# Moving the next chunk's projections, its norm and the FFN within the steps of an in-order transformer schedule

## The chip, the cores and the metric

One core of a Trainium2 chip. The metric is the device time of the whole kernel in microseconds (us), the median over its runs.

## The reference, cut to what matters

```python
# S = 2048 rows, D = 512, H = 32 heads of 16, window W = 256, Dff = 1792
def A(x):                                    # attention over a sliding window
    q, k, v = split_heads(x @ wqkv)
    scores = q @ k^T * Dh ** -0.5, masked to 0 <= i - j < W
    return (softmax(scores) @ v) @ wo
def B(x):
    return relu(x @ w1) @ w2
x = x + A(layernorm(x));  x = x + B(layernorm(x))
x = x + A(layernorm(x));  x = x + B(layernorm(x))
```

## The kernel before

The rows are cut into four chunks of 512, so two layers make eight **steps** (`k` from 0 to 7). A step has 20 **slots** (`SPS = 20`), each with one group of scores, one exponential on ACT (the scalar engine) and the matching product with V. POOL (GpSimd) and DVE (the vector engine) do masks, norms and evictions, that is, moves of results out of the matmul accumulator memory PSUM. In the gaps the tensor engine (PE) does the dense work: output projection and FFN of the chunk that is finished (`k - 1`), and the projections of the chunk that comes next (`k + 1`). Each compute engine gets its instructions in exactly the order in which the program emits them; SyncE (its issuing sequencer is SPq in the profile) issues the DMAs, also in order.

Dense work is a list of tasks. In each slot the task with the smallest `due` among those with `early <= slot` is taken, until the slot's budget of matmuls is spent; once begun, a task is finished before the next.

```python
    def plan_qkv(k, early, w0, w1):
        ...
        order = ["K0", "Q0", "V0", "K1", "V1", "Q1", "V2", "K2", "V3", "Q2", "K3", "Q3"]
        for i, what in enumerate(order):
            n = int(what[1])
            due = w0 + (w1 - w0) * (i + 1) / len(order)
            if what[0] == "K":
                Task(early, due, SPS * k + 5 * n - 3, KC, lambda n=n: k_items(layer, c, xnTs[k], n, k == 0))
            ...                                        # Q and V likewise
    # in the loop over k:
        for j in range(4):                             # norm of the next chunk, in two pairs of blocks
            at_slot(SPS * k + 5 + j, lambda k=k, j=j, fn=begin: fn(k, j))
        plan_qkv(k + 1, SPS * k + 9, SPS * k + 9, SPS * k + 20)
```

Three kinds of DMA matter. A **K group** (four in a step) leaves PSUM by ACT into a staging tile `Kst` with two buffers, and eight small copies put it into the block-diagonal `KBD`. `KBD` is a ring of 20 places: where a chunk wraps round its end (chunks 2 and 7, projected in steps 1 and 6), a group takes 16 copies. That makes 5 x 32 + 2 x 64 = 288 copies in the run. The first chunk (`direct`) is written by DVE without copies.

```python
            if not direct:
                Kst = work.tile([P, 512], BF16, name="Kst", bufs=2)
                act.copy(Kst[:], ps[0][:])
            for a, b in runs:                          # one run, or two where the ring wraps
                sa = (s0 + a) % NSLOT
                for e in range(2):
                    if direct:
                        dve.tensor_scalar(out=KBD[:, t, sa:sa + b - a, e, :], in0=ps[0]..., scalar1=par[:, e:e + 1], op0=ALU.mult)
                        continue
                    for r in range(4):
                        rows = slice(32 * r + 16 * e, 32 * r + 16 * e + 16)
                        nc.sync.dma_start(KBD[rows, t, sa:sa + b - a, e, :], Kst[rows, 64 * a:64 * b]...)
```

A **V group** (four in a step) goes by DVE to one of two staging tiles `Vst`, then by four copies to `V2f`: 112 in the run. The third kind are the **transposes**: the attention output to `OT` (four in a step, ahead of the output projection `wo`), the second norm to `xn2T` (four, ahead of the FFN) and the chunk norm to `xnT` (four, ahead of the projections). `xnT` and `xn2T` have one buffer each.

## Time and profile before

| | before |
|---|---|
| time, median of 2 runs | 674.69 us (672.6 to 676.79) |
| span, mean granted clock of the profiled run | 673.0 us, 0.844 |
| busiest engine | PE, 75% |
| K copies, V copies, transposes issued | 288, 112, 92 |

The prediction below shows how the bound was read. The "chain" in it is the work that ended last, followed back step by step to what released it; a line such as "PE 46%; SPq 12%" gives the share of the run that each engine has in that chain.

### The profile page before, as it was taken

To read this page: it belongs to the slowest core of one execution; us is meant where nothing else is said; L and a number is where in the kernel's file an instruction comes from. 1 tells how busy PE (TensorE), PEld (TensorE's weight loads), DVE (VectorE), ACT (ScalarE), POOL (GpSimd) and SP (SyncE) were. 2 spreads that over 40 slices of the span, in tenths; PEclk is the share of its full clock that TensorE was granted. 3 is DMA by queue.
4 is the path that set the end of the run, shared out by engine and by line. 5 is a ranking of instruction groups with operands and counts; after the bars stand their busy time and mean duration, and the time that the engine had idled before them with its cause. 6 is when DMAs were issued, how large, how long until landed. Compare 5 with 4: busy or idle time off the path is not lost.

```text
span 673.0 us, 14446 instructions
## 1 busy us (share of the span) xinstructions
PE 507.5 (75%) x5741; PEld 239.7 (36%) x5741; DVE 333.7 (50%) x869; ACT 317.9 (47%) x223; POOL 253.3 (38%) x558
## 2 busy tenths in 40 slices
PE   5929454797376996599958996799859586697395
PEld 2314232343132552244423442255325243344142
DVE  5662344453173646456554656364826216463451
ACT  2355673474234774367524674377626273453000
POOL 6652245431135344632453235334453221432300
PEclk8768665797786999899977997699969697699788
DMA  8511212111121112211121212112221112102201
GB/s 293 175 31 26 38 30 56 23 23 27 34 41 35 36 28 54 43 25 37 32 56 34 38 36 56 29 34 46 56 50 19 27 20 60 38 9 41 47 1 37
DMA packets 101244, 30.64 MB, mean 46 GB/s; under 512 B 85552, under 2 KB 100656, under 8 KB 101168
## 3 DMA queue, kind: packets, MB, share of 16 engines
q1 hardware_dynamic: 101168, 29.63, 20.0%
q8 instruction: 47, 0.77, 0.5%
q14 instruction: 29, 0.24, 0.1%
HBM read 7.86 MB, written 2.10 MB: 15 GB/s over the span
## 4 chain that ended last, share of the span: by engine, by line
PE 46%; DVE 14%; SPq 12%; POOL 9%; DMA 9%; issue 5%; ACT 3%; DVEq 0%; POOLq 0%; ACTq 0%
PE ps_d L94 35%; SPq L244 10%; PE acc L94 6%; PE Sps L94 5%; DMA OT<-O 4%; ACT Pb L94 3%; SPq L266 3%; DMA xnT<-xnA 3%; POOL Pb L94 3%; DVE stB L94 2%; POOL xnB L94 2%; DVE x_sb L94 2%; DVE stA L94 2%; POOL xnA L94 1%; DVE Pb L94 1%
## 5 line engine op out<-in xcount | busy, mean ns | idle before, releaser
L94 ACT ACTIVATE Pb<-Sps 128x2048 bf16<-128x2048 f32 (+2 forms) x160 | 283.4, 1771 | 207.4 <-PE Sps L94 193.3
L94 POOL TENSOR_SCALAR_AFFINE_SELECT Pb<-Pb 64x256 bf16<-64x256 bf16 x368 | 153.8, 418 | 244.5 <-ACT Pb L94 198.4
L94 PE MATMUL ps_d<-xn2T,w 128*128 128x512 bf16 x448 | 131.6, 416 | 40.8 <-DMA xn2T<-xnB 27.0
L94 DVE TENSOR_SCALAR hT<-ps_d 128x512 bf16<-128x512 f32 x112 | 77.3, 690 | 96.8 <-PE ps_d L94 96.4
L94 PE MATMUL ps_d<-w,hT 128*128 128x512 bf16 x448 | 115.9, 390 | 0.0
L94 PEld LDWEIGHTS <-Pb 128*128 128x128 bf16 x2880 | 94.0, 98 | 38.5 <-issue 14.1
L94 PE MATMUL ps_d<-xnT,wqkv 128*128 128x512 bf16 x256 | 80.9, 429 | 32.0 <-issue 16.4
L94 PE MATMUL acc<-V2f,Pb 128*128 128x34 bf16 x2880 | 95.9, 181 | 2.3 <-DVE Pb L94 1.5
L94 PE MATMUL Sps<-Qt,KBD 32*128 32x320 bf16 (+4 forms) x1408 | 67.2, 275 | 26.8 <-ACT Pb L94 25.8
L94 PE MATMUL ps_d<-wo,OT 128*128 128x512 bf16 x128 | 43.8, 470 | 48.9 <-DMA OT<-O 48.9
L94 DVE RECIPROCAL chk<-acc 128x8 f32<-128x8 f32 x128 | 26.1, 204 | 96.7 <-PE acc L94 96.0
L94 PEld LDWEIGHTS <-w 128*128 128x128 bf16 x448 | 40.2, 102 | 94.1 <-issue 57.3
L94 DVE TENSOR_TENSOR Pb<-Pb,tri 128x512 bf16<-128x512 bf16 (+1 forms) x152 | 60.4, 430 | 6.7 <-ACT Pb L94 6.5
L94 PEld LDWEIGHTS <-KBD 32*128 32x128 bf16 x1408 | 25.4, 95 | 93.1 <-issue 90.2
L94 PEld LDWEIGHTS <-hT 128*128 128x128 bf16 x448 | 38.9, 99 | 46.5 <-issue 11.4
L94 DVE TENSOR_TENSOR x_sb<-ps_d,x_sb 128x512 f32<-128x512 f32 x48 | 32.6, 688 | 43.4 <-PE ps_d L94 41.5
L94 POOL TENSOR_TENSOR rstdB<-rstdB,mhalf 128x2 f32<-128x2 f32 x16 | 11.7, 731 | 103.9 <-DVE rstdB L94 103.9
L94 ACT CAST Kst<-ps_d 128x512 bf16<-128x512 f32 x28 | 16.3, 583 | 70.8 <-PE ps_d L94 63.9
L94 PEld LDWEIGHTS <-wqkv 128*128 128x128 bf16 x256 | 23.5, 103 | 62.2 <-issue 46.0
L94 DVE TENSOR_TENSOR O<-acc,chk 128x128 bf16<-128x128 f32 x128 | 37.3, 292 | 4.4
L94 PE MATMUL ps_d<-wqkv,xnT 128*128 128x512 bf16 x128 | 36.9, 391 | 0.0
L94 DVE CAST Vst<-ps_d 128x512 bf16<-128x512 f32 x28 | 19.4, 692 | 32.3 <-DMA V2f<-Vst 25.5
(66 smaller groups left out, 253.0 us busy)
## 6 DMA issues: line engine op xcount, KB each, us to landing
V2f<-Vst SPq DMA_DIRECT2D x112, 34.0 KB, 1.9
w<-in_B_w_dram SPq DMA_DIRECT2D x2, 1792.0 KB, 13.7
KBD<-Kst SPq DMA_DIRECT2D x160, 16.0 KB, 1.9
KBD<-Kst SPq DMA_DIRECT2D x128, 8.0 KB, 1.8
out_dram<-ob SPq DMA_DIRECT2D x16, 128.0 KB, 1.7
wqkv<-in_A_wqkv_dram SPq DMA_DIRECT2D x3, 512.0 KB, 6.9
xst<-in_A_x_dram SPq DMA_DIRECT2D x3, 512.0 KB, 9.8
xst<-in_A_x_dram SPq DMA_DIRECT2D x2, 256.0 KB, 3.0
```

The lines of the kernel that those rows point to most:

```text
L94: inst = fn(*a, **k)
L244: nc.sync.dma_start(KBD[rows, t, sa:sa + b - a, e, :], Kst[rows, 64 * a:64 * b].rearrange("p (s k) -> p s k", k=64))
L266: nc.sync.dma_start(V2[64 * e:64 * e + 64, sl, e].rearrange("p a d -> p (a d)"), Vst[j % 2][64 * half:64 * half + 64, e].rearrange("p a d ...
```

## The change

The intent is to have the next chunk's projections done early, in the first half of a step, where PE has idle time; to leave the second half to the FFN of the finished chunk; and to run the next chunk's norm at the end of the step before, so that its transposes are not waited for. The diff, cut to its core:

```diff
-    def plan_qkv(k, early, w0, w1):
+    def plan_qkv(k, base):
...
-        order = ["K0", "Q0", "V0", "K1", "V1", "Q1", "V2", "K2", "V3", "Q2", "K3", "Q3"]
+        order = [("K0", 1), ("K1", 2.5), ("K2", 4), ("K3", 5.5), ("Q0", 7), ("V0", 8), ("V1", 9), ("V2", 10), ("V3", 11),
+                 ("Q1", 12.5), ("Q2", 14.5), ("Q3", 17)]
...
-                Task(early, due, SPS * k + 5 * n - 3, KC, lambda n=n: k_items(layer, c, xnTs[k], n, k == 0))
+                Task(base, base + due, base + SPS + 5 * n - 3, KC, lambda n=n: k_items(layer, c, xnTs[k], n, k == 0))
...
-        w0, w1_ = SPS * (k + 1) + 9, SPS * (k + 2) + 9          # FFN
+        w0, w1_ = SPS * (k + 1) + 9, SPS * (k + 2) + 8
...
-            at_slot(SPS * k + 5 + j, lambda k=k, j=j, fn=begin: fn(k, j))
-        plan_qkv(k + 1, SPS * k + 9, SPS * k + 9, SPS * k + 20)
+            at_slot(max(2 + j // 2, SPS * k - 4 + j), lambda k=k, j=j, fn=begin: fn(k, j))
+        plan_qkv(k + 1, SPS * k)
```

More of the change, by code (lines that the diff above doesn't have):

```diff
@@ L460, in q_make @@
             return q_items(xnTs[k], Q[k, t], t, k == 0)
-        order = ["K0", "Q0", "V0", "K1", "V1", "Q1", "V2", "K2", "V3", "Q2", "K3", "Q3"]
-        for i, what in enumerate(order):
+        order = [("K0", 1), ("K1", 2.5), ("K2", 4), ("K3", 5.5), ("Q0", 7), ("V0", 8), ("V1", 9), ("V2", 10), ("V3", 11),
+                 ("Q1", 12.5), ("Q2", 14.5), ("Q3", 17)]
+        if k == 0:
+            order = [("K0", 0), ("Q0", 0), ("V0", 1), ("V1", 1), ("V2", 1), ("V3", 1), ("K1", 2), ("Q1", 2), ("K2", 5),
+                     ("Q2", 5), ("K3", 8), ("Q3", 8)]
+        for what, due in order:
             n = int(what[1])
-            due = w0 + (w1 - w0) * (i + 1) / len(order)
             if what[0] == "K":
-                Task(early, due, SPS * k + 5 * n - 3, KC, lambda n=n: k_items(layer, c, xnTs[k], n, k == 0))
+                Task(base, base + due, base + SPS + 5 * n - 3, KC, lambda n=n: k_items(layer, c, xnTs[k], n, k == 0))
             elif what[0] == "Q":
-                Task(max(early, SPS * (k - 1) + 5 * n + 1), due, SPS * k + 5 * n - 1, KC, lambda n=n: q_make(n))
+                Task(base + 5 * n + 1 if k else 0, base + due, base + SPS + 5 * n - 1, KC, lambda n=n: q_make(n))
             else:
-                Task(max(early, SPS * (k - 1) + 7), due, SPS * k + 3, KC, lambda n=n: v_items(layer, c, xnTs[k], n, k == 0))
+                Task(base + 7 if k else 0, base + due, base + SPS + 3, KC, lambda n=n: v_items(layer, c, xnTs[k], n, k == 0))
     def plan_ffn(k, s):
@@ L519 @@
         pool.tensor_copy(x_sb[:, b, :], xst[:, b - 4, :])
-    plan_qkv(0, 0, 0, 6)
+    plan_qkv(0, -SPS)
     for k in range(NSTEP - 1):
```

## The prediction

> **What bounds the kernel now.** The schedule has eight steps (two layers, four chunks of 512 rows), each of 20 attention slots; an exponential per slot marks them, so I call the start of every twentieth one a step. From their starts in the timeline the steps of the kernel before last 60.7, 77.2, 84.5, 72.5, 69.9, 73.3, 80.7 and, with the tail, 124.9 us. I read the page first (busy shares, chain), then the list of waits, then windows of one ordinary step (245.2 to 317.7 us) cut at its slot 10, and last that step's timeline.
>
> ```profile
> span 673.0 us, 14446 instructions
> PE 507.5 (75%) x5741; PEld 239.7 (36%) x5741; DVE 333.7 (50%) x869; ACT 317.9 (47%) x223; POOL 253.3 (38%) x558
> PE 46%; DVE 14%; SPq 12%; POOL 9%; DMA 9%; issue 5%; ACT 3%; DVEq 0%; POOLq 0%; ACTq 0%
> ```
>
> No engine is full. A sixth engine shows in the chain: SPq, the sequencer that issues every DMA, with 12%.
>
> ```profile
> 245.20:289.10 43.90, 30.66 (x375) 14.48 (x374) 21.91 (x61) 20.22 (x13) 21.10 (x44) 0.88 0.21 41
> 289.10:317.70 28.60, 28.60 (x375) 14.27 (x375) 18.19 (x43) 21.43 (x16) 10.18 (x24) 1.00 0.18 32
> ```
>
> Columns: length, then PE, PEld, DVE, ACT and POOL busy, the granted clock, DMA share, GB/s. From slot 10 on PE is busy all the time at full clock, 28.6 us: nothing can be gained there. The first half holds the waits: 43.90 - 30.66 = 13.2 us of idle PE, at clock 0.88. The waits by name, over the run (us in total, times, longest):
>
> ```profile
> PE ps_d L94 <- DMA OT<-O: 48.9, 12, 10.5
> PE ps_d L94 <- DMA xn2T<-xnB: 27.0, 7, 9.6
> DVE Vst L94 <- DMA V2f<-Vst: 25.5, 5, 9.2
> PE ps_d L94 <- DMA xnT<-xnA: 15.0, 3, 7.6
> ACT Kst L94 <- DMA KBD<-Kst: 4.5, 2, 3.8
> ```
>
> And in that step's timeline (start, us, engine, work, idle before):
>
> ```profile
> 268.89 0.61 PE L94 MATMUL ps_d<-wo,OT 128*128 128x512 bf16 x1 [5.23 <-DMA OT<-O]
> ...
> 280.11 1.04 PE L94 MATMUL ps_d<-xn2T,w 128*128 128x512 bf16 x4 [2.76 <-DMA xn2T<-xnB]
> ...
> 285.70 1.01 PE L94 MATMUL ps_d<-xnT,wqkv 128*128 128x512 bf16 x2 [4.55 <-issue]
> ...
> 288.89 5.10 SPq L244 DMA_DIRECT2D KBD<-Kst  x8
> ...
> 303.17 6.00 SPq L266 DMA_DIRECT2D V2f<-Vst  x8
> ```
>
> Three transposes in turn stop PE: OT (attention output, to wo), xn2T (to the FFN), xnT (to the next chunk's projections): 12.5 of the 13.2 us. The last two lines give the price of issuing: 5.10/8 = 0.64 us for one K copy, 6.00/8 = 0.75 for one V copy (0.62 in most groups of four); transposes in the same timeline take 1.25 us each to issue. A copy lands some 1.25 us after its issue ended.
>
> **What the Trainium skill says.** "Perfetto Trace Analysis", What "DMA-bound" means: a kernel can be bound on the DMA sequencer, when the issuing engine's track is solid DMA slices, and these slices are descriptor generation, not data movement. The trace agrees: the 16 engines are 20% busy, but a step issues 32 K copies (21 us), 16 V copies (10 us) and 12 transposes (15 us), 46 of some 72 us of SPq. "DMA: Bandwidth & Descriptors", Anatomy of one DMA — SWDGE (gpsimd) path: a wait for a semaphore happens on the issuing sequencer, before dispatch. So a copy whose source isn't ready holds all later ones; SPq's waits show it. "PSUM — Partial Sum Buffer", Engine vs sequencer instructions: ScalarE, VectorE and GpSimdE are strict FIFO; so an eviction that waits for a buffer holds every exponential behind it. The waits of ACT and DVE above are of this kind. "TensorE: Matmul & The Clock Gate", Part 1: after about 3.4 us of idle PE the clock halves. The trace's clock is 1.0 or 0.5 alone, and the waits stand in the windows with 0.82 to 0.88.
>
> **The change, part by part.** No work is added or removed. The instruction order of the changed kernel, compared engine by engine, says what moves.
>
> 1. The chunk norm goes from slots 5 to 8 to the last slots of the step before. That removes the xnT wait (4.55 us above, about 4 a step) and lets the fourth OT transpose go ahead of xn2T's first pair. By the order, xnT lands about 1 to 2 us into the step, just before its first use.
>
> 2. FFN starts its second matmuls in slot 15, so by slot 0 most are done, and the projections are pulled forward: in steps 1 to 6 all four K groups are in slots 0 to 2, where K was spread over slots 9 to 19 with V and Q between. Kst has two buffers. K0 and K1 are evicted at about 5 and 5.5 us; K2's eviction waits for K0's eight copies to land: 5.6 + 8 x 0.66 + 1.2 = 12.1 us; K3's for K1's, 17.4 us. ACT is in order: the exponential of slot 3 comes behind K3, at 18.6 us, where it stood at 8.4.
>
> 3. SPq's new order is K0 K1 (16), OT0, K2 K3 (16), OT1 to OT3, xn2T (4), V (16). OT0 lands at 16.2 + 2.4 = 18.6 us, hidden behind part 2. K2 and K3 issue until 28.1; OT1 lands at 30.5, OT3 at 33.1, where before it landed at 23.7. Slot 6 starts at 33 (before: 17.4).
>
> 4. From the last wo on: addition, statistics, POOL, xn and transposes take 9 to 10 us (5.5 of DVE and POOL durations, 2.5 issue, 1.2 landing, some queueing). xn2T lands at 43.8 and PE has done slots 7 and 8 by then.
>
> 5. V's groups are in slots 7 and 8, but their copies stand behind xn2T, until 42.5. Vst has two buffers: V2's eviction waits until 42.5 + 2.5 + 1.25 = 46.3, V3's until 48.8, and DVE is in order, so the accumulators of slot 8 and the first relu wait too. PE has four such PSUM tiles: its second FFN group waits for V2's, its third for V3's. Slot 10 starts at about 50.5 (before: 43.9).
>
> 6. From slot 10 on nine large matmuls a slot as before: 28 us. An ordinary step: 50.5 + 27.5 = 78 us, with step 4 (smaller exponentials) 76.
>
> 7. Split steps 1 and 6: the ring wraps, and each K takes 16 copies, 64 in all, 42 us. Step 1 has 48 ahead of OT0: K2 can be evicted at 14.6, K3 at 25.1, OT0 lands at 37, OT1 at 48.5 (16 more). Its OT3 also stands behind xn2T's first pair: 59. Last wo 60, xn2T 68.5, V until 73.5, slot 10 at 75.5: step 103 us. Step 6 (32, OT0, 32): OT3 at 53.7, xn2T 64.4, slot 10 at 71: 98 us. In return step 2 loses the spill of step 1's copies (84.5 becomes 78), and step 7, which projects nothing, that of step 6's: it had a slot of 11.9 us behind them; slots 0 to 8 now take 24 us, xn2T is there at 29, eleven slots of 3.15 follow: 64 for 71.8.
>
> 8. Step 0: K0 of the next chunk is in slot 4, but xnT has one buffer, so its transposes wait for the last Q of this chunk: 13 us, plus 5 issuing, plus 1.2. K copies issue from 21 to 42 us, V after that; V3's eviction is at 48.6, two units of 11 us are left: 70 (before 60.7).
>
> Sum of differences: step 0 +9.3, step 1 +25.8, step 2 -6.5, steps 3 to 5 +5.5 +6 +5, step 6 +17.5, step 7 -8: **+54.6 us on 674.7, 729 us**. All these times are estimates by hand from the durations above.
>
> **The rivals.** (a) The intended gain: the transposes' waits vanish and nothing replaces them. For it: PE's three waits in the list make 91 us; the norm does leave the critical place. Against: the OT and xn2T waits depend on SPq, and its order puts all K copies before OT. If half of the 91 us went, 629. (b) A trade at par: K's burst fills time in which PE has other work, as ACT has slack (47% busy), and the lost xnT wait pays for the rest. For it: first-half PE work is only some 30 of 43.9 us. Against: wo and FFN depend on each other, there are just 72 matmuls to put in between, and those stand in order behind the wait. It would give 665 to 690. (c) Worse than the sum: longer idle stretches halve the clock for more of the first half, and DVE, behind by 5 us at slot 10, keeps FFN groups waiting for PSUM. 750 to 765.
>
> **Range and chances.** I trust the sign: it comes from the order on a queue whose durations are measured. The size hangs on the split steps (43 of the 55 us) and on step 0. If half of the K burst were hidden, 700; with (c), 760. So 729, 8 in 10 in 698 to 760; faster 0.04, same 0.06, slower 0.90.
>
> **What would show it.** Right: waits of Kst for KBD grow from 4.5 us to over 60 (in an ordinary step 4 + 5, in a split one about 8 + 10, each with its 20 us or so of late exponentials); Vst for V2f from 25.5 to about 40; the OT wait from 48.9 to 70 or more; xnT below 10; steps 1 and 6 near 100 us, steps 2 and 7 shorter; no group's mean duration changed but by the clock. Wrong: steps 1 and 6 not longer than 85 us, or a first half below 44 us with K's copies still ahead of OT; then copies issue faster when the queue is full than the groups of eight show, or the evictions don't wait.

## More of the kernel before

Besides, two lines of the table of DMA issues and two of the table of groups are needed later. The first two give the tiles, the count, the size and the time from issue to landing; the others give count, busy us, mean ns, and after the second bar the idle time before the group and what ended it.

```profile
KBD<-Kst SPq DMA_DIRECT2D x160, 16.0 KB, 1.9
KBD<-Kst SPq DMA_DIRECT2D x128, 8.0 KB, 1.8
...
L94 PE MATMUL ps_d<-wo,OT 128*128 128x512 bf16 x128 | 43.8, 470 | 48.9 <-DMA OT<-O 48.9
...
L94 ACT CAST Kst<-ps_d 128x512 bf16<-128x512 f32 x28 | 16.3, 583 | 70.8 <-PE ps_d L94 63.9
```

The reader should see that ACT's evictions of K wait for the matmuls that make K, not for copies: before the change the staging buffers are nearly always free in time.

## The result, and the profile after

The changed kernel took 774.21 us (median of 2 runs, 773.59 to 774.82) for 674.69. A ratio in this text is the mean time of one kernel's fast runs over the mean of the fast runs of the kernel before from the same rounds, so not quite the ratio of the two medians. Here it is 1.1475, with a 95% interval of 1.1316 to 1.1633: slower by some 15%. The experiments' own runs of the kernel before had medians of 674.1 to 674.9 us.

The page of the kernel after, in the same order as the lines of before in the prediction and above: span, busy time, engines of the chain that ended last, then the two groups.

```profile
span 773.1 us, 14419 instructions
...
PE 527.7 (68%) x5741; PEld 242.7 (31%) x5741; DVE 330.2 (43%) x869; ACT 317.1 (41%) x223; POOL 254.2 (33%) x558
...
PE 36%; SPq 22%; POOL 12%; DVE 11%; DMA 9%; issue 6%; ACT 3%; ACTq 0%; DVEq 0%; POOLq 0%
...
L94 PE MATMUL ps_d<-wo,OT 128*128 128x512 bf16 x128 | 49.8, 541 | 102.6 <-DMA OT<-O 102.2
...
L94 ACT CAST Kst<-ps_d 128x512 bf16<-128x512 f32 x28 | 16.0, 587 | 98.3 <-DMA KBD<-Kst 79.3
```

The counts are the same, 5741 matmuls and 28 evictions of K, and DVE, ACT and POOL are busy for the same time within 4 us. PE alone is busy 20 us longer, with the same instructions: its mean clock fell from 0.844 to 0.807. The issuing sequencer's share of the chain rose from 12% to 22%. The waits by name:

```profile
PE ps_d L94 <- DMA OT<-O: 102.2, 15, 18.2
ACT Kst L94 <- DMA KBD<-Kst: 79.3, 14, 9.7
DVE Vst L94 <- DMA V2f<-Vst: 53.8, 8, 13.0
PE ps_d L94 <- DMA xnT<-xnA: 33.1, 7, 9.7
PE ps_d L94 <- DMA xn2T<-xnB: 25.4, 7, 10.0
```

Four of the five grew, by 53, 75, 28 and 18 us; only xn2T's stayed. The windows of one ordinary step of the kernel after, cut at its slot 10 as before (columns as in the prediction):

```profile
294.20:351.40 57.20, 35.74 (x375) 15.45 (x374) 17.93 (x51) 21.81 (x17) 17.18 (x37) 0.77 0.23 40
351.40:380.20 28.80, 28.80 (x375) 14.31 (x374) 21.24 (x55) 19.73 (x13) 13.80 (x32) 0.99 0.12 16
```

The second half is as it was (28.8 us for 28.6). The first half has 57.2 - 35.7 = 21.5 us of idle PE for 13.2, and 5.1 us more of busy PE for the same 375 matmuls, at clock 0.77 for 0.88. The loss of an ordinary step is in its first half. Here is how it comes about, in the timeline of the next step, which starts at 380.19 (start, us, engine, work, idle before):

```profile
380.54 1.81 POOL L94 TENSOR_SCALAR xnA<-x_sb,rstdA,nbA 128x512 bf16<-128x512 f32 x2
...
385.49 0.59 PE L94 MATMUL ps_d<-xnT,wqkv 128*128 128x512 bf16 x2 [3.74 <-DMA xnT<-xnA]
...
388.34 10.84 SPq L244 DMA_DIRECT2D KBD<-Kst  x16
...
399.28 1.22 SPq L346 DMA_TRANSPOSE OT<-O  x1
400.59 10.39 SPq L244 DMA_DIRECT2D KBD<-Kst  x16
400.66 0.59 ACT L94 CAST Kst<-ps_d 128x512 bf16<-128x512 f32 x1 [4.60 <-DMA KBD<-Kst]
...
401.78 1.89 PE L94 MATMUL ps_d<-wo,OT 128*128 128x512 bf16 x4 [8.10 <-DMA OT<-O]
...
411.08 3.84 SPq L346 DMA_TRANSPOSE OT<-O  x3
413.57 3.43 PE L94 MATMUL ps_d<-wo,OT 128*128 128x512 bf16 x8 [3.88 <-DMA OT<-O]
```

Read the SPq lines alone: 16 copies, one transpose, 16 copies, three transposes, without a gap. The transposes that PE waits for stand behind the copies. Read then the first two lines: the norm's last pair is on POOL only after the step has begun, so the first projection waits 3.74 us. All lengths of steps in this text are read the same way, from the start of every twentieth exponential:

| step | 0 | 1 | 2 | 3 | 4 | 5 | 6 | 7 and tail |
|---|---|---|---|---|---|---|---|---|
| before | 60.7 | 77.2 | 84.5 | 72.5 | 69.9 | 73.3 | 80.7 | 124.9 |
| predicted | 70 | 103 | 78 | 78 | 76 | 78 | 98 | 117 |
| after | 72.7 | 111.8 | 87.3 | 86.0 | 82.7 | 87.1 | 103.7 | 113.0 |

### The profile page after: what moved, and what is told of

It is laid out like the page before. It is cut to its first block, busy times and chain, and to the rows that moved or that the text cites. A ratio compares the mean times of both kernels' runs of the same rounds, so it can differ in the third digit from the quotient of the medians.

```text
span 773.1 us, 14419 instructions
## 1 busy us (share of the span) xinstructions
PE 527.7 (68%) x5741; PEld 242.7 (31%) x5741; DVE 330.2 (43%) x869; ACT 317.1 (41%) x223; POOL 254.2 (33%) x558
## 4 chain that ended last, share of the span: by engine, by line
PE 36%; SPq 22%; POOL 12%; DVE 11%; DMA 9%; issue 6%; ACT 3%; ACTq 0%; DVEq 0%; POOLq 0%
PE ps_d L94 28%; SPq L244 18%; PE acc L94 5%; POOL Pb L94 4%; PE Sps L94 4%; DMA OT<-O 4%; POOL xnA L94 3%; SPq L266 2%; DMA xnT<-xnA 2%; POOL xnB L94 2%; ACT Pb L94 2%; DVE stB L94 2%; DMA V2f<-Vst 2%; SPq L199 2%; DVE x_sb L94 1%
## 5 line engine op out<-in xcount | busy, mean ns | idle before, releaser
L94 PE MATMUL ps_d<-xn2T,w 128*128 128x512 bf16 x448 | 128.7, 423 | 39.4 <-DMA xn2T<-xnB 25.4
L94 PE MATMUL ps_d<-wo,OT 128*128 128x512 bf16 x128 | 49.8, 541 | 102.6 <-DMA OT<-O 102.2
L94 PE MATMUL ps_d<-w,hT 128*128 128x512 bf16 x448 | 118.7, 395 | 0.8 <-DVE x_sb L94 0.8
L94 PE MATMUL ps_d<-xnT,wqkv 128*128 128x512 bf16 x256 | 81.5, 445 | 37.4 <-DMA xnT<-xnA 33.1
L94 PE MATMUL Sps<-Qt,KBD 32*128 32x320 bf16 (+4 forms) x1408 | 67.6, 276 | 43.2 <-ACT Pb L94 42.1
L94 ACT CAST Kst<-ps_d 128x512 bf16<-128x512 f32 x28 | 16.0, 587 | 98.3 <-DMA KBD<-Kst 79.3
L94 PEld LDWEIGHTS <-OT 128*128 128x128 bf16 x128 | 13.1, 121 | 126.4 <-DMA OT<-O 109.1
L94 DVE CAST Vst<-ps_d 128x512 bf16<-128x512 f32 x28 | 19.3, 690 | 67.0 <-DMA V2f<-Vst 53.8
```

Source lines behind the costliest of these rows:

```text
L94: inst = fn(*a, **k)
```

## The experiments

Two kinds of name recur: "the kernel after" is the changed one, "norm early" the kernel after with its norm two slots earlier. Each kernel was run in three rounds, on the same chip as runs of the kernel before. All outputs are right. Rounds of different experiments ran on different chips, so ratios are safer than differences where a few us count. Two things were to be settled: which of the waits makes the loss (theory: the K copies' issue time on SPq, ahead of OT; rivals: the two `Kst` buffers, which hold ACT; the late norm), and why the loss is 45 us more than predicted.

### 1. The kernel after without K copies

```diff
-  ... lambda n=n: k_items(layer, c, xnTs[k], n, k == 0))
+  ... lambda n=n: k_items(layer, c, xnTs[k], n, True))
```

> The changed kernel, but every K group is evicted by DVE straight into its block-diagonal place (two masked copies, or four where the ring wraps, as step 0 of both kernels does for the first chunk); the 32 to 64 copies a step and Kst are gone from the DMA queue. Queue theory (K's copies stand ahead of OT, and their two staging buffers hold ACT): the waits for OT fall from 102 to under 25 us, Kst's waits are gone, steps 1 and 6 are no longer than 2 to 5 (about 65 us each), and the whole is about 600 to 630 us although DVE does some 40 us more. Rival, the norm's place or the clock costs the time: OT waits fall, but the total stays above 720.

Measured: 627.96 us, ratio 0.9296 (0.9271 to 0.9321), 146 us less than the kernel after, for 38 us more of DVE. From its page the chain, and from its waits the one for OT:

```profile
PE 44%; DVE 19%; POOL 16%; DMA 9%; SPq 4%; issue 4%; ACT 2%; DVEq 0%; POOLq 0%; ACTq 0%
...
PE ps_d L94 <- DMA OT<-O: 15.3, 10, 6.2
```

SPq's share fell from 22% to 4%, the wait for OT from 102 to 15 us. Without K copies the new order beats the kernel before (experiment 2 has the fair comparison, with the same edit in both). One part of the expectation failed: step 1 still takes 79.4 us, where about 65 was expected; step 6 takes 66.9.

### 2. The same in the kernel before

The same edit in the kernel before's own task line.

> The kernel before with the same direct eviction of K. Queue theory: the K3 copies no longer stand ahead of OT, the split steps 1, 2 and 6 lose their extra 10 to 15 us, xnT and xn2T waits stay. About 635 to 655 us. If the copies were hidden there: 670 or more, as DVE has more to do.

Measured: 630.71 us, ratio 0.9336 (0.9308 to 0.9363), a little below the range. So the same 288 copies cost 674.7 - 630.7 = 44 us in the order before and 774.2 - 628.0 = 146 us in the order after: 0.15 and 0.51 us each, for 0.64 to 0.71 us of issue in bursts of sixteen. The difference, 102 us, is as large as the whole loss; what is left of the change comes out even (628.0 for 630.7, within the spread of the runs). Experiment 10 shows that "even" hides a gain and a cost.

### 3. Four Kst buffers

```diff
-                Kst = work.tile([P, 512], BF16, name="Kst", bufs=2)
+                Kst = work.tile([P, 512], BF16, name="Kst", bufs=4)
```

To make room, the norm's `xn` has two buffers for three and the softmax check's tile one for two.

> The changed kernel with four staging buffers for K in place of two (the memory is taken from one xn buffer and one chk buffer). The order of the DMA queue is the same. ACT theory (exponentials behind K2's and K3's evictions set the step): Kst's wait for KBD falls from 79 to under 10 us and the time falls by 60 us or more, to about 700. Queue theory (OT stands behind the copies whatever ACT does): Kst's wait goes, the OT wait grows by about as much as the exponentials come earlier, and the time is 755 to 774 us.

Measured: 774.23 us, ratio 1.1483 (1.1453 to 1.1513): no change. The list of waits has no line "Kst <- DMA KBD<-Kst" any more, where it had 79.3 us, and in its place:

```profile
PE ps_d L94 <- DMA OT<-O: 135.6, 15, 26.7
```

Most of ACT's 79 us had not held PE: PE's waits for the exponentials (Sps for Pb) fell only from 42.1 to 12.9 us. These 29 us are found again here, where the wait for OT grew by 33. In an ordinary step slot 3 came at 14.0 us for 22.6, but slot 10 at 57.8 for 57.2. The wait of ACT is real and long, yet it was not what set the time; PE arrived sooner and waited longer. With the smaller side buffers this is not quite a one-part experiment, but the only wait of that kind in its list is POOL's for `xn`, 4.5 us in all, too little to hide a gain of 79.

### 4. Norm two slots earlier

```diff
-            at_slot(max(2 + j // 2, SPS * k - 4 + j), ...
+            at_slot(max(2 + j // 2, SPS * k - 6 + j), ...
```

> The changed kernel with the chunk norm two slots earlier (14 to 17 in place of 16 to 19). The prediction had xnT landing 1 to 2 us into a step; it landed at 5.1, and PE idled 3.7 us for it in steps 2 to 6. If this is a term of its own, each of steps 1 to 6 loses 3 to 4 us, the xnT wait falls from 33 to about 12 us and the time by 20 to 25 us, to about 750. If OT's place in the queue hides it, the xnT wait falls, the OT wait grows by as much, and the time stays within 1%.

Measured: 749.37 us, ratio 1.1102 (1.1057 to 1.1147), 25 us less than the kernel after. The wait for xnT falls from 33.1 us in 7 times to 10.4 in two, 9.7 of it in step 0:

```profile
PE ps_d L94 <- DMA OT<-O: 107.4, 15, 19.7
...
PE ps_d L94 <- DMA xnT<-xnA: 10.4, 2, 9.7
```

An ordinary step has its slot 1 at 2.5 us for 6.4, and slot 10 at 53.1 for 57.2. The late norm costs 25 us; of what was taken away, 5 us came back at OT.

### 5. K groups later in the step

```diff
-        order = [("K0", 1), ("K1", 2.5), ("K2", 4), ("K3", 5.5), ...
+        order = [("K0", 6.1), ("K1", 6.3), ("K2", 6.5), ("K3", 6.7), ...
```

K tasks may also not start before slot 6.

> The changed kernel with K's groups from slot 6 on in place of slots 0 to 2, so that OT and xn2T go ahead of nearly all K copies in the DMA queue; their number is the same. If OT's place in the queue is the cost: OT's wait falls from 102 to under 40 us and the time to about 680. If it is the queue's time, wherever it is put in a bunch: the 21 us (42 in steps 1 and 6) then stand ahead of V's copies, the wait of Vst for V2f grows from 54 to 130 us or more, ACT still waits for Kst, and the time is 740 to 780 us.

Measured: 743.15 us, ratio 1.1038 (1.0982 to 1.1094), inside the low end of the range.

```profile
DVE Vst L94 <- DMA V2f<-Vst: 122.6, 13, 27.2
ACT Kst L94 <- DMA KBD<-Kst: 105.4, 14, 14.8
PE Sps L94 <- ACT Pb L94: 97.9, 28, 13.3
...
PE ps_d L94 <- DMA OT<-O: 13.8, 10, 6.6
```

OT hardly waits any more (13.8 us), yet only 31 us are won, and most of these are not due to the copies: as K starts later, the late norm isn't waited for either (the wait for xnT is 12.8 us, for 33.1 in the kernel after and 10.4 with norm early). Against norm early, 749.37 us, the gain is 6 us. The same burst of copies now stands ahead of V's: the wait has moved to V's and K's evictions, and through ACT to the scores (Sps). In these two places a burst of 32 copies costs about the same.

### 6. ACT issues the K copies (a miss)

```diff
-                        nc.sync.dma_start(KBD[rows, t, sa:sa + b - a, e, :],
+                        act.dma_start(KBD[rows, t, sa:sa + b - a, e, :],
```

> The changed kernel with the K copies issued by ACT in its own order, not by SP. SP's queue is then as empty as with direct eviction: OT's waits under 30 us. If issuing is the cost, ACT pays it: 32 x 0.65 us ahead of the exponential of slot 3, ACT's own stream shows gaps of 5 us a K, and the time is 715 to 745 us, far above the 628 of direct eviction. If only SP's order mattered: below 650 us.

Measured: 821.05 us, ratio 1.2197 (1.2139 to 1.2256), the slowest of all, where 715 to 745 was expected. ACT's timeline in an ordinary step (step 3, which starts at 314.2) shows why; ACTq is ACT's own sequencer:

```profile
322.98 6.09 ACTq L94 DMA_DIRECT2D KBD<-Kst  x8
329.17 0.59 ACT L94 CAST Kst<-ps_d 128x512 bf16<-128x512 f32 x1 [6.22 <-DMA KBD<-Kst]
329.79 5.44 ACTq L94 DMA_DIRECT2D KBD<-Kst  x8
335.33 1.88 ACT L94 ACTIVATE Pb<-Sps 128x2048 bf16<-128x2048 f32 x1 [5.57 <-DMA KBD<-Kst]
```

ACT does nothing while its sequencer issues: an eviction of K and an exponential each stand behind eight copies. The OT wait is indeed gone (9.5 us), but the exponentials of slots 1, 2 and 3 are 14.7 and 13.9 us apart, and the wait of the scores for ACT rises from 42 to 159 us. The expectation had foreseen the gaps of 5 us, but put their sum at 87 to 117 us above experiment 1. Measured are 821.1 - 628.0 = 193 us, or 0.67 us a copy, as much as its whole issue. ACT's work (an exponential a slot) is needed by every slot, so on balance none of the issue was hidden.

### 7. Norm early in the kernel before

```diff
-            at_slot(SPS * k + 5 + j, lambda k=k, j=j, fn=begin: fn(k, j))
+            at_slot(SPS * k + (1 if k else 5) + j, lambda k=k, j=j, fn=begin: fn(k, j))
```

> The kernel before with one part of the change alone, the chunk norm earlier (slots 1 to 4 of the same step in place of 5 to 8; the last slots of the step before aren't to be had, as the last Q still reads xnT there). If the norm's place is worth the xnT wait: that falls from 15 us plus the 4.5 us issue gaps to near 0, some 4 us a step: 645 to 660 us. If the next wait in line (xn2T) takes its place: 668 to 680 us.

Measured: 658.72 us, ratio 0.9777 (0.9729 to 0.9825), within the expected range; the interval excludes 1, but not a gain below 2%. The wait for xnT falls from 15.0 to 7.6 us, that for OT rises from 48.9 to 64.0. An earlier norm, which the change also intended, is thus worth about 15 us in the order before.

### 8. Half of the K copies (a miss)

K0 and K1 written by DVE, K2 and K3 by copies (`k == 0 or n < 2`), in the kernel after.

> The changed kernel with K0 and K1 evicted directly and K2 and K3 by copies: half of the copies, 16 a step (32 in steps 1 and 6), still in slots 0 to 2. Queue theory: the copies then begin some 2 us later than K0's did and are through 11 us after (21 in split steps); in steps 1 and 6 OT0 and OT1 to OT3 still stand behind them, in the others the 11 us fall mostly beside slots 2 to 4, so more than half of the 146 us between 774 and 628 goes: 650 to 680 us, with an OT wait of 30 to 60 us. If the loss were in proportion to the number of copies: 701.

Measured: 700.23 us, ratio 1.0395 (1.0362 to 1.0427). I had expected the copies of K0 and K1 to cost more than those of K2 and K3 (650 to 680 us). They don't: taking away the one half gives 74 us and then the other 72, and the middle of 628.0 and 774.2 is 701.1. The issuing queue in its step 3, which starts at 263.8, shows the reason:

```profile
274.81 1.19 SPq L346 DMA_TRANSPOSE OT<-O  x1
276.96 11.14 SPq L244 DMA_DIRECT2D KBD<-Kst  x16
288.20 3.84 SPq L346 DMA_TRANSPOSE OT<-O  x3
```

The first OT is free now, but the 16 copies stand between it and the other three. The wait for OT is still 75.9 us. In this order each copy ahead of the last OT costs its share.

### 9. K copies spread out

The kernel after with all 288 copies, norm early, and the K groups in slots 8, 11, 13 and 15, behind the transposes and with V and Q between:

```diff
-        order = [("K0", 1), ("K1", 2.5), ("K2", 4), ("K3", 5.5), ...
+        order = [("K0", 9.5), ("K1", 12), ("K2", 14), ("K3", 16), ...
```

> The changed kernel with all its K copies, but K's groups spread over slots 8, 11, 13 and 15 in place of slots 0 to 2, and the norm two slots early. The queue's slack theory: a copy costs time only where it is issued in a bunch ahead of something PE waits for; between slots 8 and 19 it is hidden beside FFN matmuls, as in the kernel before. Then the OT wait is under 40 us and the time 615 to 645 us, the rest over 602 being steps 1 and 6, whose 42 us don't fit. Rival, each copy costs 0.5 us wherever it stands (as the half and the full set of copies did): about 745.

Measured: 632.48 us, ratio 0.9385 (0.9359 to 0.9411), inside the expected range.

```profile
PE ps_d L94 <- DMA OT<-O: 13.8, 8, 6.7
```

The wait for OT is 13.8 us for 107.4 with norm early. Ordinary steps take 60.7 to 64.2 us; those with 64 copies, or with the spill of such a step (1, 2 and 6), still take 74 to 83. The same copies that cost 148 us in a burst (norm early, 749.4, against 601.7 of the next experiment) cost 31 us here. Against norm early the edit changes nothing but the slots of the K groups. So it is their place, and not their number, that made the loss.

### 10. The parts put together

Four kernels: K direct with norm early in the order after, K direct with the norm in slots 1 to 4 in the order before, norm early with V direct alone, and K and V direct with norm early.

> Direct eviction of K and the norm two slots earlier together. If the two terms add: 628 - 25 = 603 us, with no wait for xnT in steps 1 to 6. If the xn2T wait takes over: 615 to 628.

> The kernel before with direct eviction of K and the norm in slots 1 to 4: all but the reordering of projections and FFN. If that reordering is worth something once the copies are gone, this stays above the 602 us of the changed kernel with the same two edits: 610 to 620. If it is worth nothing: 598 to 606.

> The changed kernel with direct eviction of K and V and the early norm; no copies are left on the queue but the first loads and the output. The wait of Vst for V2f (46 us on DVE, of which PE feels 12) goes; DVE does 4 V evictions of 4 x 0.42 us in place of 0.69, about 4 us more a step, in the slots before the first relu. If the waits were what counted: 585 to 598. If DVE's work takes their place: 600 to 610.

> The kernel after with its norm two slots earlier and V written straight from PSUM by the vector engine, so that V's 112 copies are gone while K's 288 stay as they are. Theory: V's copies stand behind the transposes of xn2T on the issuing queue (in step 1 until 81.2 us, where the prediction had 73.5), hold V's third and fourth eviction, and with them the first FFN groups, for 3 to 6 us a step: 715 to 735 for 749; steps 1 to 6 each shorter before their slot 10. Rival: V's copies lie beside work that would not have been ready in any case: 742 to 752.

| kernel after, norm early | with V copies | without V copies |
|---|---|---|
| with K copies | 749.37 (1.1102) | 721.76 (1.0680; 1.0631 to 1.0729) |
| without K copies | 601.69 (0.8927; 0.8871 to 0.8984) | 577.42 (0.8562; 0.8526 to 0.8597) |

Both rows and columns add up: K copies cost 148 us with V's and 144 without, V copies 28 and 24. The norm is worth 25 us with K copies (774.2 to 749.4) and 26 without (628.0 to 601.7). In the order before, K direct with the norm early gave 616.03 (0.9138; 0.9101 to 0.9176), so the order after is 14 us better once no K copies stand in it and the norm is early; the norm's place is not the same in the two, so this is not the order alone. This makes up the account of the loss: the K copies cost 102 us more in the order after (experiment 2), the norm's place costs 26 us there and 15 in the order before (630.7 to 616.0), and the rest gains 14: 102 + 12 - 14 = 100, for a measured 99.5. The last cell beats both kernels by far, and did better than its expected range. Its page:

```profile
PE 473.1 (82%) x5648; PEld 232.0 (40%) x5741; DVE 395.6 (69%) x1025; ACT 302.6 (53%) x195; POOL 255.5 (44%) x558
...
PE 57%; DVE 22%; DMA 8%; POOL 5%; issue 4%; ACT 2%; SPq 1%; DVEq 0%; POOLq 0%; ACTq 0%
```

The span of the profiled run is 576.3 us. DVE took 65 us more of work than in the kernel after (395.6 for 330.2) and was still only 69% busy. (This trace lacks 93 of the 5741 matmul records, so its PE busy time is a little low.)

### 11. PE kept busy in the waits

To see whether half clock explains the rest of the miss, dummy matmuls (425 in all) were put ahead of the output projections that wait for OT. They overwrite a PSUM tile that the projection then starts anew.

```diff
                 ps.append(ps_d.tile([P, 512], FP32, name="ps_d"))
+                for _ in range(fill):
+                    mm(ps[0][:], ident[:], ident[:].rearrange("p (o q) -> p o q", o=1).to_broadcast([P, 4, P]), True, True)
```

> The kernel after with its norm two slots earlier, and with dummy matmuls (identity times identity, 128x512, 0.21 us each at full clock) put on the tensor engine just before the output projections that wait for OT in steps 1 to 6: as many as fill each wait seen in the run without them (40 and 18 in an ordinary step, 85 and 62 in step 6, 425 in all). They write the PSUM tile that the projection then overwrites, so the result is the same. Theory (what is left of the miss, 749 against a predicted 729, is half clock after the waits): the eight output projections behind the second wait take 1.7 us for 3.4, xn2T lands about 2 us sooner in each of six steps, so 735 to 741. Rival (the clock is lost beside the waits of the issuing queue, and the rest of the miss lies in the chain of norm and transposes and in the V copies): 746 to 752, with the mean of the wo group back near 390 ns all the same.

> The same dummy matmuls in the kernel after itself, its norm where the change puts it. Theory of the half clock: 758 to 766 for 774. Rival: 771 to 777, as the issuing queue sets when OT lands and the norm's own wait stays.

Measured: norm early with the dummies 746.79 us (1.1042; 1.0983 to 1.11) for 749.37; the kernel after with them 770.58 (1.1413; 1.1366 to 1.1459) for 774.21. The dummies did their work in the main, as the wait for OT (25.5 us for 107.4) and the clock show (0.876 for 0.807); from the first kernel's page:

```profile
L94 PE MATMUL ps_d<-wo,OT 128*128 128x512 bf16 x115 | 36.6, 441 | 26.0 <-DMA OT<-O 25.5
```

Yet at most 3 to 4 us came of it, and the intervals overlap with those without dummies, so the theory of the half clock (735 to 741, and 758 to 766) falls, and its rival holds in the main. The dummies did not hold up the projections themselves: in steps 1 to 6 none of the recorded ones began more than 0.7 us after its OT had landed. In step 3 the fourth xn2T transpose was issued by 43.5 us after the step's start for 44.7, but the sixteen V copies behind it took 11.0 us for 10.2, and ended at 54.6 for 55.0. There the queue took what the clock gave. The expectation that the group's mean would be back near 390 ns was missed: it is 441, as in steps 3, 4 and 6 six, six and eleven of the projections still ran at half clock (over 600 ns), behind the waits that were left. So it is the part of the half clock that the dummies took away that is worth so little; the part that stayed was not tested. (13 of the 128 records of this group are missing from the trace.)

## Why the prediction was right or wrong

**The sign and its cause were right.** Rival (a), the intended gain, and rival (b), a trade at par, were both off: four of the five waits grew. The step that carried the prediction, the order on SPq with all K copies ahead of OT (part 3), is shown by experiments 1, 2 and 9: the copies cost 102 us more than before, where the whole difference is 99.5, and by their place. The times of part 3 hold to the microsecond once the norm is out of the way: in step 3 with norm early, OT0 landed at 18.2 us (predicted 18.6), OT1 at 30.5 (30.5), OT3 at 33.5 (33.1).

**The size was wrong: 729 us, range 698 to 760, measured 774.** The step that failed first is part 1, "By the order, xnT lands about 1 to 2 us into the step, just before its first use". It landed about 5.1 us into it. By the order of instructions the norm stood in slots 16 to 19, but its second pair on POOL comes behind that slot's affine selects (2.9 us) and behind the statistics, which DVE finishes in slot 18. PE lost 3.7 us to it in the step shown, and slot 1 came 3.9 us later in an ordinary step. The prediction thus put this term at zero; it measured 25 us over the run (experiment 4), the larger part of the 45 us that were missing. The expectation "xnT below 10" failed with it (33.1).

**The other 20 us** are spread. With norm early, the steps take 73.0, 110.0, 80.9, 81.6, 78.8, 81.1, 99.9 and 112.8 us, which is +3, +7, +2.9, +3.6, +2.8, +3.1, +1.9 and -4.2 against the prediction. The landings in the trace of norm early say where they arise:

- Part 4 is too short. Between the landing of the last OT and that of the last xn2T the prediction had 9.5 us in step 1 and 10.7 in steps 3 and 6; measured are 11.6, 12.5 and 12.2. With the dummies of experiment 11 it is 10.5, 10.9 and 12.2, so in steps 1 and 3 half or more of what part 4 lacks went away with the half clock.
- Parts 5 and 7 held from there on: from xn2T's landing to slot 10 the prediction had 6.6 to 7.0 us, the steps 1 to 6 take 6.6 to 7.3. So the copies of V cost 28 us in all with norm early (experiment 10), but no more by slot 10 than had been allowed for them, even though part 7 had those of step 1 issued until 73.5 us and the last was issued at 81.2. Slot 10 was late by 4.0 us in step 1 and by 1.8, 2.6 and 1.7 in the ordinary steps 2, 3 and 5, nearly all of it before xn2T's landing.
- The second half of steps 1, 2, 3 and 5 was 28.5 to 30.5 us where part 6 had 27.5; before it was already 28.6.
- Step 0: part 8 had xnT landing at about 19 us and the copies of K from 21 us; the queue stood 2.6 us for the norm's second pair, xnT landed at 22.9, and the copies began at 25.5. This fits the 3 us of the step, but no run tests it.

Rival (c), which gave 750 to 765 for half clock and for DVE being late, named the right direction, but what the dummies took away of the half clock gave only 3 to 4 us (experiment 11), although PE is busy 20 us longer. In the trace with dummies slot 10 comes 0.3 to 2.0 us earlier in steps 1 to 4, but later in 5 and 6, and steps 2 and 3 lose the gain in their second half. Why they do, and what makes second halves 1 us and more longer than part 6, stays open.

**Part 2** (ACT held by two Kst buffers) was right as a description: the wait of Kst for KBD is 79.3 us, "over 60". It was wrong as a cost: the prediction let it set slot 3 and called the landing of OT0 hidden behind it. Experiment 3 shows that the landing sets the time with or without it: with the wait gone the time is the same (774.23 for 774.21 us).

**The rest of the list.** The OT wait (102.2, predicted 70 or more), steps 1 and 6 (near 100; 111.8 and 103.7) and the shorter step 7 (113.0 for 124.9) held. Vst for V2f was 53.8 where about 40 was named. Step 2 was not shorter (87.3 for 84.5; 80.9 with norm early, so it was the norm again). That no group's mean duration changed but by the clock is seen in the group lines: the evictions of K took 587 ns for 583, the wo matmuls 541 for 470.

**What the skill's pages said.** That a kernel can be bound on the sequencer that issues its DMAs ("Perfetto Trace Analysis", What "DMA-bound" means) was the reading that found the sign. The same page's DMA Optimizations say that balancing DMAs over the engines that can issue them may help in that case; here it made things worse, 821 for 774 us, since the other engine had work of its own in the path. What helped was to have no such DMAs, or to issue them where nothing waits behind them.

## What to carry to other kernels

An in-order DMA issuer is an engine like any other: before work is pulled forward, write down its queue in the new order with the measured time of each issue, and look at what the critical transposes will stand behind. Here a burst of small copies cost three quarters of its issue time where critical transfers stood behind it (0.51 us a copy), and a sixth where it was spread behind such transfers (0.11 us); a spare compute engine that wrote the destination straight from PSUM was cheaper than either. And a norm "in the slot before" lands when its slowest engine's queue is through: look at that queue too. Here two slots more were enough.

## What the Trainium skill lacked or had wrong

- "DMA: Bandwidth & Descriptors", Issuing engines are not separate DMA queues, says of the time to initiate a DMA on a sequencer that it is "usually small relative to the DMA itself". Here one K copy takes 0.64 to 0.71 us to issue and 1.8 to 1.9 us from issue to landing, so issue is over a third; with 288 of them in a bad place the copies cost 146 of 774 us.
- "Perfetto Trace Analysis", DMA Optimizations, advises to balance DMAs over the issuing engines without naming the price: ACT's evictions and exponentials stood still for 5.2 to 6.1 us per eight copies, and the kernel went from 774 to 821 us.
- No page gives, for this chip by name, the time that the issuing sequencer is held by one DMA of each kind ("DMA: Bandwidth & Descriptors" has only cycle counts for unnamed earlier generations). The runs show 0.64 to 0.71 us for a copy of 8 or 16 KB from one tile to another, 0.62 to 0.75 for a V copy of 34 KB, and 1.2 to 1.3 us for a transpose.
- "TensorE: Matmul & The Clock Gate", Part 1, has the halved clock after idle windows, and the trace agrees (3.43 us for eight wo matmuls behind a wait, 1.68 us for seven FFN matmuls in a busy stretch; mean clock 0.81). It doesn't say that undoing much of it can be worth next to nothing: raising the mean clock from 0.81 to 0.88 with dummy matmuls gave at most 3 to 4 us of 774, within the spread of the runs.
